# Moving the buffers of a TensorE-filled kernel to other offsets modulo 512 bytes

## The chip, the cores and the metric

The kernel runs on one NeuronCore of one Trainium2 chip. The metric is the device time of one execution in microseconds (us). A program that runs on one core has one span, and the profile shows one execution of it.

## The reference

Three layers follow one another, all in float32: a sparse attention, and two gated feed-forward layers on its output.

```python
def _attn_ref(q, k, v):                      # each 4 x 8 x 576 x 64
    scores = scale * np.matmul(q, k.transpose(0, 1, 3, 2))
    rel = pos[:, None] - pos[None, :]
    mask_local = (rel >= 0) & (rel < 32)                       # heads 0 to 3
    mask_strided = (rel >= 0) & (pos[None, :] % 32 == pos[:, None] % 32)   # heads 4 to 7
    ...
    return np.matmul(attn, v)                # softmax of the masked scores, times v

def _moe_ref(x, w_a, w_b, w_out):            # x 2304 x 512, w_a and w_b 512 x 1536
    return (x @ w_a) * (x @ w_b) @ w_out

def _moe2_ref(x, w_gate, w_val, w_out):      # the same shapes
    return 1.0 / (1.0 + np.exp(-(x @ w_gate))) * (x @ w_val) @ w_out
```

The result is `_moe2_ref(_moe_ref(_attn_ref(q, k, v)))`, 2304 tokens by 512.

## The kernel before, in words

**Precision.** Every large product is made of three matmuls in float32r, a 4-byte type that TensorE takes at one column per cycle: high part of the weights by high part of the data, low by high, high by low. So each operand lies in SBUF twice, as a high and a low part. The stationary operand of a matmul (its weights) is always 128 by 128; the moving operand is 512, 384 or 256 columns wide. Each matmul has its own weight load, and the load of the next matmul runs while the current one streams.

**Stages.** (1) Tokens come in five tiles: four of 512 columns (128 positions of 4 sequences) and a last one of 256. For each tile the attention is computed (local heads on TensorE at L569, L610 and L624, strided heads by VectorE at L787 to L857, their transposes at L883), and then the first layer runs over 12 slices of its inner dimension: per slice 24 matmuls at L929 (two products of 4 chunks by 3 parts) and 12 at L1020 (the output product). That gives 4 x 12 x 24 = 1,152 matmuls at L929 and 4 x 12 x 12 = 576 at L1020 that are 512 wide, and 288 and 144 that are 256 wide. Attention and strided heads of the next tile run beside the first layer of the current one. (2) The second layer's gate and value products, and (3) its output product, use a seven-product scheme for blocks of two by two; all their matmuls are 384 wide and issue from L1299: 3 x 6 x 14 x 6 = 1,512 in stage 2 and 3 x 14 x 18 = 756 in stage 3, 2,268 in all. At the very start, while there is little to do, TensorE is fed with bf16 matmuls of zeros (L429, tile `nil`), 512 wide.

**Order.** A planner (`Plan`) sorts all operations of all engines by costs and due times before anything is issued, and the program is written out in that order. TensorE's large matmuls are tied in one chain by `chain`.

**Memory.** SBUF is addressed by column numbers. The columns up to F0 are cut into 17 zones: `w0` to `w11` of 12,288 bytes per partition, which hold the first layer's weights; `x12` to `x15` of 8,192 bytes, which hold the tokens (`x12`, `x13` high parts, `x14`, `x15` low parts); and `h16` of 4,096 bytes for the features between the first layer's two products. In stages 2 and 3 the same zones hold weights and moving operands of the second layer, in other roles. What lies behind F0 is in one tile, `rest`. The function `at` turns a column number into a view, and makes a zone's tile (`sb.tile`, with one tag per zone) when the zone is first used. The allocator packs tiles in the order in which they are first made.

**Start addresses.** All pieces inside the zones begin at multiples of 512 bytes from the zone's start, with one exception: the tokens and features of the last, 256 wide, tile begin 192 bytes further (`SHIFT = 48` columns, in `token_column` and `gated`). In the kernel before, every zone begins at 384 modulo 512 bytes. So the first column of a moving operand and the first column of the weights that are loaded meanwhile have the same address modulo 512 in all 512 and 384 wide matmuls, and are 192 bytes apart in the 256 wide ones. Below, that distance (moving operand's start minus the start of the next matmul's weights, modulo 512) is called the offset.

Of the kernel before, what the change touches and what calls it, by code (L numbers as in the profile page):

```python
# [7 lines left out]
F32 = mybir.dt.float32  # L8
# [14 lines left out]
P = 128  # L23
KC = DM // P
KF = DFF // P
# [44 lines left out]
REGIONS = [(i * ZONE, ZONE) for i in range(KF)]  # L70
# [3 lines left out]
REGIONS += [(H0, 2 * N2)]  # L74
F0 = H0 + 2 * N2
EARLY, FIRST, SECOND, THIRD = range(4)
RINGS = {"c": (8, DM), "qk": (2, QW + KW), "g": (1, N2), "raw": (3, T * D), "hh": (1, N2), "hl": (1, N2)}
PLACE, TOP = {"hh": H0, "hl": H0 + N2}, F0
for _n, (_k, _w) in RINGS.items():
    if _n not in PLACE:  # L80
# [4 lines left out]
def region_of(a):  # L85
    return next((r for r in REGIONS if r[0] <= a < r[0] + r[1]), None)
# [86 lines left out]
class Plan:  # L173
# [39 lines left out]
    def add(self, eng, cost, fn, deps=(), key=0.0, take=(), free=(), size=0):  # L213
# [7 lines left out]
        for ring, owner in free:  # L221
            if ring in PLACE:
                taker, i = owner if isinstance(owner, tuple) else (owner, None)
                rings = [allowed for r, allowed in taker.take if r == ring]
                for allowed in rings if i is None else rings[i:i + 1]:
                    size = RINGS[ring][1]
                    for s in allowed:
# [124 lines left out]
def attention_moe_kernel(ctx, tc, qkv, sq, sk, sv, w1, w2, mask, ident, out):  # L352
# [4 lines left out]
    sb = ctx.enter_context(tc.tile_pool(name="sb", bufs=1))  # L357
# [10 lines left out]
    tiles = {}  # L368

    def at(a, n, phase=FIRST, dtype=F32):  # L370
        r = region_of(a)
        if r is None:
            v = rest[:, a - F0:a - F0 + n]
        else:
            if tiles.get(r, (None,))[0] != phase:
                name = f"{('w', 'x', 'h')[(r[0] >= X0) + (r[0] >= H0)]}{REGIONS.index(r)}"
                tiles[r] = phase, sb.tile([P, r[1]], F32, tag=name, name=f"{name}p{phase}")
            v = tiles[r][1][:, a - r[0]:a - r[0] + n]
        return v if dtype == F32 else v.bitcast(dtype)

    def xT(i, c):

        return at(X0 + (2 * i + c // 2) * XZONE, XZONE, FIRST, F32R).rearrange("p (c n) -> p c n", c=HK)
# [5 lines left out]
    def buf(op, ring, shape, dtype=F32):  # L389
        s = op.slot[ring][0]  # L390
        if ring in PLACE:
            return at(PLACE[ring] + s * RINGS[ring][1], shape[1], FIRST, dtype)
        return sb.tile(shape, dtype, tag=f"{ring}{s}", name=f"{ring}{s}")
# [65 lines left out]
    def convert(w, need, start=()):  # L459
# [3 lines left out]
        def clear(op):  # L463
            for i in op.slot["c"]:
                tops.append(at(PLACE["c"] + i * DM, DM, FIRST, U32))
                POOL.memset(tops[-1], 0)
# [567 lines left out]
    for i, n in enumerate(TILES):  # L1034
        n *= B
        war = reads1[-1:]
        w = [g for g in GROUPS if g.i == i + 1]
# [563 lines left out]
```

## Time and profile before

| what | value |
|---|---|
| median of 2 runs | 903.11 us (902.96 to 903.26) |
| the profiled execution | 902.92 us, of which 901.1 us is the span from the first to the last instruction |
| TensorE (PE) busy | 892.8 us, 99% |
| VectorE (DVE) busy | 655.1 us, 73% |
| ScalarE (ACT) busy | 405.0 us, 45% |
| DMA | 132.67 MB, 147 GB/s on average |

PE stands for TensorE's matmuls, PEld for its weight loads, which overlap them. A matmul's duration in the profile is its way through the array and not the time that it costs in a row of matmuls: that time is the distance between the starts of two of them, and it can be read where the chain that ended last lists a number of matmuls with their joint time.

### The profile page before, as it was taken

How to read it: one execution, taken by the hardware profiler on the slowest of the kernel's cores; microseconds unless marked ns; L12 is line 12 of the kernel's file. 1: busy time of each engine (PE TensorE's matmuls, PEld its weight loads, DVE VectorE, ACT ScalarE, POOL GpSimd, SP SyncE). 2: the span in 40 equal slices, each digit the busy share in tenths (PEclk: the TensorE clock that was granted, in tenths of full speed). 3: DMA queues.
4: the chain of work that ended last, by engine and by line, in shares of the span. 5: the costliest groups of instructions: out<-in, count | busy, mean ns of one | idle time of the engine just before them, and what ended most of it. 6: DMA issues, size and time to landing. Idle time of an engine off the chain costs nothing.

```text
span 901.1 us, 13664 instructions
## 1 busy us (share of the span) xinstructions
PE 892.8 (99%) x5170; PEld 802.0 (89%) x5170; DVE 655.1 (73%) x1078; ACT 405.0 (45%) x843; POOL 11.4 (1%) x23
## 2 busy tenths in 40 slices
PE   8999999999999999999999999999999999999998
PEld 4678888888888888888899999999999999999998
DVE  7999988998999879811328876675768458649481
ACT  5776644411242113311236655564656445435351
POOL 4000000000000000000000000000000000000000
PEclk9999999999999999999999999999999999999999
DMA  9676564311242124300034233645575588953501
GB/s 297 212 238 221 200 195 141 91 44 61 85 137 72 54 65 134 106 1 1 0 118 164 94 139 116 213 152 187 204 241 169 194 302 331 381 165 117 167 17 62
DMA packets 62513, 132.67 MB, mean 147 GB/s; under 512 B 5872, under 2 KB 37232, under 8 KB 61552
## 3 DMA queue, kind: packets, MB, share of 16 engines
q1 hardware_dynamic: 62160, 131.60, 43.7%
q8 instruction: 40, 0.66, 0.3%
q14 instruction: 25, 0.20, 0.1%
q10 hardware_dynamic: 288, 0.21, 0.1%
HBM read 97.19 MB, written 34.60 MB: 146 GB/s over the span
## 4 chain that ended last, share of the span: by engine, by line
PE 97%; DVE 3%; issue 0%; ACT 0%; DVEq 0%
PE bank L1299 43%; PE bank L929 33%; PE bank L1020 17%; PE bank L624 1%; PE idle L429 1%; PE bank L569 1%; PE bank L610 1%; PE bank L883 0%; DVE nm L581 0%; DVE rest L497 0%; PE bank L442 0%; DVE w8p L857 0%; DVE w9p L857 0%; DVE x14p L636 0%; DVE w4p L1255 0%; DVE w0p L509 0%
## 5 line engine op out<-in xcount | busy, mean ns | idle before, releaser
L954 ACT CAST h16p<-rest 128x512 fp32r<-128x512 f32 (+1 forms) x60 | 34.7, 578 | 143.7 <-PE bank L1020 140.5
L1311 DVE TENSOR_TENSOR rest<-bank,rest 128x384 f32<-128x384 f32 x84 | 46.3, 555 | 56.6 <-PE bank L1299 32.5
L950 DVE TENSOR_TENSOR rest<-bank,rest 128x512 f32<-128x512 f32 (+1 forms) x60 | 38.1, 635 | 53.7 <-PE bank L929 53.5
L1072 ACT COPY rest<-bank 128x512 f32<-128x512 f32 (+1 forms) x60 | 32.6, 544 | 92.2 <-PE bank L929 92.0
L1317 ACT COPY rest<-bank 128x384 f32<-128x384 f32 x84 | 40.2, 479 | 67.4 <-PE bank L1299 67.1
L958 DVE TENSOR_TENSOR h16p<-rest,h16p 128x512 fp32r<-128x512 f32 (+1 forms) x60 | 38.2, 636 | 28.8 <-PE bank L1020 23.5
L787 DVE TENSOR_TENSOR rest<-rest 128x320 f32<-128x320 f32 (+13 forms) x56 | 51.5, 920 | 1.3 <-DMA rest<-sq 0.5
L850 DVE TENSOR_TENSOR rest<-rest,s 128x320 f32<-128x320 f32 (+13 forms) x56 | 51.5, 920 | 0.9
L793 DVE TENSOR_REDUCE s<-rest 128x5 f32<-128x320 f32 (+13 forms) x56 | 51.2, 915 | 1.2
L857 DVE TENSOR_REDUCE rest<-rest 128x64 f32<-128x320 f32 (+13 forms) x56 | 51.2, 915 | 1.0
L488 ACT ACTIVATE rest<-rest 128x512 f16<-128x512 bf16 x36 | 28.4, 793 | 9.4 <-DMA rest<-w 9.1
L1209 DVE SCALAR_TENSOR_TENSOR rest<-rest 128x512 uint32<-128x512 uint32 x36 | 24.7, 688 | 9.9 <-ACT rest L1202 9.8
L1202 ACT ACTIVATE rest<-rest 128x512 f16<-128x512 bf16 x36 | 28.0, 788 | 5.5 <-DMA rest<-w 5.5
L1382 DVE TENSOR_TENSOR rest<-bank,rest 128x384 f32<-128x384 f32 x36 | 20.0, 556 | 12.1 <-PE bank L1299 11.4
L1321 ACT COPY bank<-bank 128x384 f32<-128x384 f32 x42 | 19.6, 466 | 18.6 <-PE bank L1299 18.3
L1376 ACT ACTIVATE rest<-bank 128x384 f32<-128x384 f32 x36 | 17.6, 490 | 22.3 <-PE bank L1299 22.1
L497 DVE SCALAR_TENSOR_TENSOR rest<-rest 128x512 uint32<-128x512 uint32 x36 | 24.5, 685 | 0.6 <-ACT rest L488 0.5
L587 ACT ACTIVATE rest<-bank,nm 128x96 f32<-128x96 f32 x56 | 18.3, 338 | 12.2 <-DVE nm L582 10.7
L1376 ACT ACTIVATE rest<-rest 128x768 f32<-128x768 f32 x18 | 15.2, 846 | 14.0 <-DVE rest L1311 13.7
L1299 PE MATMUL bank<-w8p,w10p 128*128 128x384 f32 x100 | 20.7, 334 | 0.0
L1382 DVE TENSOR_TENSOR rest<-rest 128x768 f32<-128x768 f32 x18 | 17.2, 954 | 0.7 <-ACT rest L1376 0.3
L1299 PEld LDWEIGHTS bank<-w8p,w10p 128*128 128x128 f32 x100 | 17.6, 188 | 0.0
(500 smaller groups left out, 2413.7 us busy)
## 6 DMA issues: line engine op xcount, KB each, us to landing
rest<-w SPq DMA_DIRECT2D x72, 511.8 KB, 3.9
h2d<-rest SPq DMA_DIRECT2D x18, 768.0 KB, 4.2
rest<-qkv SPq DMA_DIRECT2D x12, 416.0 KB, 4.0
w2p<-h2d SPq DMA_DIRECT2D x12, 384.0 KB, 4.6
w0p<-h2d SPq DMA_DIRECT2D x12, 384.0 KB, 5.0
w1p<-h2d SPq DMA_DIRECT2D x12, 384.0 KB, 5.5
out<-rest SPq DMA_DIRECT2D x24, 192.0 KB, 1.8
x2d<-rest SPq DMA_DIRECT2D x16, 256.0 KB, 2.1
```

Of the source, the lines that this page charges most:

```text
L787: engine[op.eng].tensor_tensor(out=product(op, n), in0=x["k", h][:, :, :n, :], in1=x["q"][h // 2][:, e:e + nh, j:j + 1, :].to_broadcast([P ...
L793: DVE.tensor_reduce(out=weights_of(h, j, n), in_=x["p", op.deps[0]], op=ALU.add, axis=AX.X)
L850: engine[op.eng].tensor_tensor(out=product(op, n, "p (h d t) -> p h d t"), in0=x["v", h][:, :, :, :n], in1=weights_of(h, j, n).unsqueeze(2 ...
L857: DVE.tensor_reduce(out=xs[:, j, e:e + nh, :], in_=x["p", op.deps[0]], op=ALU.add, axis=AX.X)
L929: PE.matmul(x[tag][:, :n], ww[:, c * P:(c + 1) * P], xx(c), start=(u == 0 and c == chunks[0]), stop=(u == last and c == chunks[-1]),)
L950: DVE.tensor_tensor(out=x["g"], in0=x["b"][:, :n], in1=x["g"], op=ALU.mult)
L958: DVE.tensor_tensor(out=x["hl"], in0=x["g"], in1=r32(x["hh"]), op=ALU.subtract)
L1020: PE.matmul(ps[:, :n], ww[:, m * P:(m + 1) * P], x[xx], start=start, stop=stop)
L1299: PE.matmul(bank_of(where), at(*lhs(a, (0, 1, 0)[q], c), F32R), at(*rhs(b, (0, 0, 1)[q], c), F32R), start=p in OPENS and (q, c) == units[0 ...
L1311: DVE.tensor_tensor(out=at(*o), in0=bank_of("Z"), in1=at(*a), op=ALU.add)
L1317: "ACT", act2(NS), lambda op: ACT.copy(out=at(*o), in_=bank_of("Y")), [ops[after]], key - 20))
L1382: DVE.tensor_tensor(out=at(*o), in0=src(), in1=at(*o), op=ALU.mult)
```

## The change

The zones are made ahead of everything else, in a fixed order (`PLACED`), and some of them get a few columns more than they use (`PADS`), so that the next zone begins elsewhere modulo 512 bytes. All columns are used as before, and each engine executes the same instructions, in the same order and with the same waits; only addresses differ. `FRONT`, which is 0, adds nothing.

```diff
@@ -74,6 +74,11 @@
 EARLY, FIRST, SECOND, THIRD = range(4)
+PLACED = ["x12", "x13", "x14", "h16", "x15"] + [f"w{i}" for i in range(KF)]
+PADS = {"x12": 48, "x13": 32, "h16": 32} | {f"w{i}": 16 for i in range(7)}
+FRONT = 0
@@ -374,9 +379,14 @@
-                tiles[r] = phase, sb.tile([P, r[1]], F32, tag=name, name=f"{name}p{phase}")
+                tiles[r] = phase, sb.tile([P, r[1] + PADS.get(name, 0)], F32, tag=name, name=f"{name}p{phase}")
...
+    if FRONT:
+        sb.tile([P, FRONT], F32, name="front")
+    for name in PLACED:
+        at(REGIONS[int(name[1:])][0], 1, EARLY)
```

The allocation that follows, start modulo 512 bytes:

| zone | before | after |
|---|---|---|
| x12, x13 (tokens, high) | 384, 384 | 0, 192 |
| x14, x15 (tokens, low) | 384, 384 | 320, 448 |
| h16 (features) | 384 | 320 |
| w0, w1, w2, w3 | 384 each | 448, 0, 64, 128 |
| w4, w5, w6 | 384 each | 192, 256, 320 |
| w7 to w11 | 384 each | 384 each |

Counted over the program, the offset of a matmul to the weights loaded behind it falls out like this after the change (in per cent of the matmuls of that width; before, 100% at 0, 100% at 0 and 100% at 192):

| offset | 0 | 64 | 128 | 192 | 256 | 320 | 384 | 448 |
|---|---|---|---|---|---|---|---|---|
| 512 wide | 8 | 12 | 16 | 8 | 8 | 16 | 8 | 23 |
| 384 wide | 18 | 12 | 16 | 17 | 11 | 11 | 6 | 9 |
| 256 wide | 16 | 8 | 23 | 8 | 12 | 16 | 8 | 8 |

## Rows read from the trace of the kernel before

**Rows 1.** The page: busy time per engine, and the TensorE clock granted per slice.
```profile
span 901.1 us, 13664 instructions
...
PE 892.8 (99%) x5170; PEld 802.0 (89%) x5170; DVE 655.1 (73%) x1078; ACT 405.0 (45%) x843; POOL 11.4 (1%) x23
...
PEclk9999999999999999999999999999999999999999
```

**Rows 2.** The page: the chain that ended last, by engine and by line.
```profile
PE 97%; DVE 3%; issue 0%; ACT 0%; DVEq 0%
PE bank L1299 43%; PE bank L929 33%; PE bank L1020 17%; PE bank L624 1%; PE idle L429 1%; PE bank L569 1%; PE bank L610 1%; PE bank L883 0%; DVE nm L581 0%; DVE rest L497 0%; PE bank L442 0%; DVE w8p L857 0%; DVE w9p L857 0%; DVE x14p L636 0%; DVE w4p L1255 0%; DVE w0p L509 0%
```

**Rows 3.** The chain in order of time, stage 1: start us, us, what.
```profile
440.50 5.44 PE bank L929 x24
445.94 2.72 PE bank L1020 x12
...
479.65 2.83 PE bank L929 x24
482.48 1.41 PE bank L1020 x12
```

**Rows 4.** The same, stages 2 and 3, the two longest pieces.
```profile
503.01 43.70 PE bank L1299 x252
551.57 346.26 PE bank L1299 x1996
```

**Rows 5.** The same, the bf16 matmuls of zeros, 7.3 to 9.2 us.
```profile
7.23 2.16 PE idle L429 x10
```

**Rows 6.** The same, four float32 transposes at 170 us.
```profile
170.62 0.44 PE bank L610 x4
```

**Rows 7.** Busy time in stretches: us, then busy us (x count) of PE, PEld, DVE, ACT, POOL, clock, DMA.
```profile
25.00:75.00 50.00, 48.39 (x325) 37.83 (x325) 47.44 (x97) 36.42 (x87) 0.00 (x0) 1.00 0.70 224
75.00:130.00 55.00, 55.00 (x247) 45.54 (x246) 53.10 (x97) 33.24 (x53) 0.26 (x1) 1.00 0.57 191
130.00:240.00 110.00, 110.00 (x603) 90.19 (x602) 99.41 (x142) 31.31 (x82) 0.31 (x1) 1.00 0.31 95
...
552.00:740.00 188.00, 188.00 (x1087) 188.00 (x1086) 120.79 (x239) 107.14 (x209) 0.00 (x0) 1.00 0.60 203
```

**Rows 8.** Weight loads (PEld) of two lines: busy us, mean ns of one.
```profile
L1299 PEld LDWEIGHTS bank<-w8p,w10p 128*128 128x128 f32 x100 | 17.6, 188 | 0.0
...
L883 PEld LDWEIGHTS bank<-idt,rest 128*128 128x128 f32 x28 | 3.5, 140 | 1.1
```

**Rows 9.** The chain in order of time between the two pieces of rows 4.
```profile
546.74 0.56 DVE rest L1311
...
550.29 1.23 DVE w4p L1255
```

## Prediction

> **What bounds the kernel now.** I read the page first. TensorE is busy for 892.8 of 901.1 us and its clock is granted in full in every slice [rows 1], so this is a kernel that ends when TensorE has worked off its matmuls. The chain that ended last says the same by line: L1299, L929 and L1020, the three lines with the float32r matmuls, hold 93% of the span, and everything on VectorE together 3% [rows 2]. No idle time is left to win and no instruction is moved. So the change can act in one way only: through the time that one matmul takes from its start to the start of the next.
>
> That time stands in the chain in order of time, where a run of matmuls has a count and a joint time. L929 with 512 columns: 5.44 us for 24, or 226.7 ns; L1020 with 512 columns: 2.72 for 12, the same. In the last tile, with 256 columns, 2.83 for 24 is 117.9 and 1.41 for 12 is 117.5 [rows 3]. Stages 2 and 3: 346.26 us for 1,996 is 173.5 ns at 384 columns, and 43.70 for 252 is 173.4 [rows 4]. At the full clock, 2.4 GHz by the granted clock, the columns alone take 213.3, 160.0 and 106.7 ns. What a matmul costs beyond its columns is then 13.4 ns at 512, 13.5 ns at 384, and 11.0 ns at 256. For a yardstick, the bf16 matmuls of zeros, also 512 wide, take 2.16 us for 10, or 216.0 ns: 2.7 ns beyond their columns [rows 5]. So float32r pays some 10.7 ns per matmul that bf16 does not pay, and the question of this case is how much of it hangs on where the two operands lie.
>
> **The change, part by part.** It removes, adds and moves no instruction, no transfer and no wait, so none has a price; that part is 0. Of the 17 zones 12 (x12 to x15, h16, w0 to w6) get another place modulo 512, and for the matmuls that matter the offset between moving operand and next weights stops being 0: 92% of the 1,728 matmuls of 512 columns and 82% of the 2,268 of 384 columns go to another offset, while 16% of the 432 of 256 columns, now at 192, go to 0. The other engines read and write the same zones at other places too; with VectorE at 73% and ScalarE at 45% [rows 1] I cost that at nothing, and TensorE's work hides it.
>
> *The price of the offset.* The trace has one pair of rows in which it differs: 512 and 384 columns run at offset 0 and pay 13.4 and 13.5 ns, 256 columns run at 192 and pay 11.0 [rows 3, 4]. The first two are alike although their widths differ by 128 columns, so a price by width does not offer itself, and a lower price by offset does: 2.4 to 2.5 ns per matmul. The bounds are wide. No gain: the 256 wide matmul may owe its 11.0 ns to its width alone. Largest gain: all that bf16 does not pay, 10.7 ns at 512, 10.8 at 384 and, for the matmuls of the last tile that find a cheap offset, 8.3. Loss: nothing excludes that other offsets cost more than 0 does, since only 192 was ever run. I take the value from the nearest rows, 2.4 ns, because they are the same instruction with the same load beside it; the bf16 rows differ in type and have zeros as data.
>
> Sum by that value: 1,728 x 0.92 x 2.4 = 3.8 us, and 2,268 x 0.82 x 2.5 = 4.6 us; back go 432 x 0.16 x 2.4 = 0.2 us. That is 8.2 us. Set against the profiled execution (901.1 us span, 1.8 us around it, 902.9 in all) it leaves 894.7, and against the median of 903.1 it leaves 895.
>
> *What could eat the gain.* In the first tiles VectorE is nearly full too: 47.44 of 50 and 53.10 of 55 us [rows 7]. A TensorE that is 1% faster needs 104 instead of 105 us there, against 100.5 us of VectorE, so the gain stays; one that is 4.7% faster (10.7 of 226.7 ns) needs 100 us and meets VectorE's own work. From 130 us on VectorE has 10% of room, and in stage 2 a third [rows 7]. Between the two long runs of L1299 the chain goes through VectorE and ScalarE for 4.9 us [rows 4, 9]; that stretch gains nothing, which is 0.05 us.
>
> **The rivals.** *A: part of the cost goes, as above,* 895 us.
>
> *B: the offset is no cost.* Weight load and moving operand may never meet. For it: the four transposes in a row at 170 us follow each other at 110 ns [rows 6], with weights that lie 384 bytes apart in turn, so at four different offsets to the same moving identity, and the other transposes look the same; nor do the weight loads say anything of being stretched, 188 ns each [rows 8]. Against it: a float32 transpose takes those 110 ns for 128 columns, half the pace, so its moving operand leaves every second slot free, and its load takes 140 ns, not 188 [rows 8]; and the 13.4 and 13.5 against 11.0 ns stay unexplained. The time is that of now, 903. The Trainium skill ("SBUF — State Buffer", Who interferes with whom, and the section on the bandwidth pool) says this outright: TensorE has one read port for the moving operand and another for weight loads, and never waits on anyone. By that rule the change does nothing, 903 us; the float32r rows, which pay 10.7 ns that bf16 does not, do not refute it, since the type could cost that by itself.
>
> *C: nearly all of the cost goes.* Two streams that start at the same place modulo 512 bytes, 3,996 times, is what a collision would need to be at its worst, and then only 18% or less of the matmuls would keep it. For it: the 256 wide matmul, at 117.5 ns, may be held by something else, such as its own weight load, which at 188 ns is longer than the whole distance [rows 8], so that its 11.0 ns hides a price of the offset that is lower still. Whole: 1,728 x 0.92 x 10.7 = 17.0, 2,268 x 0.82 x 10.8 = 20.1, 432 x 0.84 x 8.3 = 3.0, together 40.1 us, less some 2 us for VectorE's full stretch: 865. Half of it: 884. Against it: the seven other offsets would all have to be cheap. The Trainium skill's price for a matmul of 512 columns in a row ("TensorE: Matmul & The Clock Gate", Back-to-back issue gap) is N / 2.4 + 2.5, or 215.8 ns, which is what the bf16 rows show and the float32r rows do not.
>
> *D: other offsets are dearer than 0, and it gets slower.* The place is the weight load beside a stream. With offset 0 both start together, and the moving operand, which takes a column per cycle, draws ahead of a load that needs longer; if it starts behind the load's place instead (offsets 256 to 448), it would run into it. Those offsets hold 55% of the 512 wide and 37% of the 384 wide matmuls. Were they to pay the 13.4 ns twice: 1,728 x 0.55 x 13.4 + 2,268 x 0.37 x 13.5 = 12.7 + 11.3 = 24 us, 927 us. It decides from 4.5 ns more per matmul on (18 us over 3,996). For it: nothing in the rows prices those offsets. Against it: the one other offset that was run, 192, is cheaper and not dearer.
>
> That the change does not do what it says is no rival: the allocation shows the places.
>
> **How the numbers follow.** A 0.34, B 0.30, C 0.24, D 0.12. The prediction is A's 895. The range has to hold 8 in 10: A and B and the nearer part of C, from 868 (C's whole effect, less a little) to 906 (B with 0.3% of noise and secondary effects); left out are D's larger part and the last bit of C, about 0.19. What a measurement of this kernel can tell from no change is taken as 2%, 18 us: faster than 885 is nearly all of C and none of A, 0.24; slower than 921 is D's larger part, 0.10; the rest, with A and B in it, is 0.66.
>
> **What would show it right or wrong.** After the change, the joint times in the chain are the test. A: L929 with 24 of 512 columns takes 5.38 to 5.40 us in place of 5.44, and L1299 shows 171 to 172 ns; slices where tokens and weights happen to keep offset 0 (w1 against x12, w4 against x13, w6 against h16) stay at 226.7. B: all rows as they were. C: slices below 5.3 us, and between 25 and 130 us waits of TensorE for VectorE. D: distances that differ from slice to slice, some over 230 ns. I would be most wrong if the distance depended on the absolute place of one operand and not on the offset between two, since then the one pair of rows that I price from says nothing about the other places.

## The result, and the profile after

The changed kernel takes 913.33 us (912.74 to 913.91, 2 runs) against 903.11: a ratio of 1.0113, with a 95% interval of 1.0070 to 1.0157. It is slower by 10.2 us, where 8.2 us less had been forecast, and outside the range of 868 to 906.

The page of the kernel after (busy time per engine, granted clock per slice) shows that TensorE's own time grew: its matmuls are busy for 902.5 us in place of 892.8, with the same number of them and the full clock, while VectorE and ScalarE stay within 1 us of before [rows 1].

```profile
span 911.0 us, 13664 instructions
...
PE 902.5 (99%) x5170; PEld 804.9 (88%) x5170; DVE 655.9 (72%) x1078; ACT 405.3 (44%) x843; POOL 11.6 (1%) x23
...
PEclk9999999999999999999999999999999999999999
```

The chain that ended last, in order of time, is where the time can be seen (start us, us, what). The file is ten lines longer, so L929, L1020 and L1299 are now L939, L1030 and L1309. First some slices of stage 1, then one of the last tile, then stages 2 and 3:

```profile
191.50 5.55 PE bank L939 x24
197.05 2.77 PE bank L1030 x12
...
205.37 2.72 PE bank L1030 x12
...
214.08 2.80 PE bank L1030 x12
216.88 5.54 PE bank L939 x24
...
490.78 2.87 PE bank L939 x24
493.64 1.42 PE bank L1030 x12
...
510.01 44.05 PE bank L1309 x252
...
558.94 348.70 PE bank L1309 x1996
```

Before, 24 product matmuls took 5.44 us in every undisturbed slice and 12 output matmuls 2.72 [rows 3]. Now the products take 5.54 to 5.55, and the output matmuls depend on the slice: 2.77 with the weights of `w5` (offset 64), 2.72 with `w6` (offset 0), 2.80 with `w7` (offset 448). So the same instruction, in the same program, with its features in the same place, has three prices, and at offset 0 it has its old one. The product matmuls are another matter: their offset changes every two matmuls, and those at offset 0 or 256 among them do not keep the old price. By the distances of their starts (stalls over 260 ns left out), 175 such matmuls took 231.4 ns on average, hardly another time than those at offset 64 (230.2), 128 (231.4) and 192 (232.3), all modulo 256. In the last tile the prices scatter around the old ones (2.87 for 2.83, 1.42 for 1.41). Stage 1 ends 7.0 us later (the first run of L1309 starts at 510.01 instead of 503.01), and the two runs of stages 2 and 3 are 0.35 and 2.44 us longer [rows 4]; that is 9.8 of the 9.9 us by which the span grew. The chain through VectorE and ScalarE between them [rows 9] lasts 4.9 us as it did, and TensorE's waits are those of before.

### The profile page after: what moved, and what is told of

Read it like the earlier page. It is cut to its first block, busy times and chain, and to the rows that moved or that the text cites. A ratio compares the mean times of both kernels' runs of the same rounds, so it can differ in the third digit from the quotient of the medians.

```text
span 911.0 us, 13664 instructions
## 1 busy us (share of the span) xinstructions
PE 902.5 (99%) x5170; PEld 804.9 (88%) x5170; DVE 655.9 (72%) x1078; ACT 405.3 (44%) x843; POOL 11.6 (1%) x23
## 4 chain that ended last, share of the span: by engine, by line
PE 97%; DVE 3%; issue 0%; ACT 0%; DVEq 0%
PE bank L1309 43%; PE bank L939 33%; PE bank L1030 17%; PE bank L634 1%; PE idle L439 1%; PE bank L579 1%; PE bank L620 1%; PE bank L893 0%; DVE nm L591 0%; DVE rest L507 0%; PE bank L452 0%; DVE w8p L867 0%; DVE w9p L867 0%; DVE x14p L646 0%; DVE w4p L1265 0%
## 5 line engine op out<-in xcount | busy, mean ns | idle before, releaser
L1309 PE MATMUL bank<-w8p,w10p 128*128 128x384 f32 x100 | 20.8, 336 | 0.0
L1309 PEld LDWEIGHTS bank<-w8p,w10p 128*128 128x128 f32 x100 | 17.7, 188 | 0.0
L1309 PE MATMUL bank<-x15p,w3p 128*128 128x384 f32 x88 | 17.5, 336 | 0.0
```

Of the source, the lines that this page charges most:

```text
L1309: PE.matmul(bank_of(where), at(*lhs(a, (0, 1, 0)[q], c), F32R), at(*rhs(b, (0, 0, 1)[q], c), F32R), start=p in OPENS and (q, c) == units[0 ...
```

## The experiments

Three theories were set against each other. *Pair*: a matmul's time is set by the offset between its moving operand and the weights beside it. *Place*: it is set by where an operand lies by itself, or by the new order of the zones. *Switch*: it is the change of the offset from one matmul to the next that costs, and not the offset. All runs use the changed kernel's fixed order of zones unless the text says otherwise. Those with tokens and features mapped to other offsets, the one without the shift and the two with a shift of a few columns were executed once, the others 4 to 10 times; all but one of the 33 times of the kernel before that were taken beside them lie between 902.46 and 904.57, so a difference of a microsecond in one execution says nothing. The kernel before had a median of 903.02 us beside the first four (19 runs), 902.46 beside the next four (one run), and 903.42 beside the last four (13 runs).

**All zones at another place, offset 0.**

```diff
-PADS = {"x12": 48, "x13": 32, "h16": 32} | {f"w{i}": 16 for i in range(7)}
-FRONT = 0
+PADS = {}
+FRONT = 48
```

> All 17 zones begin at 192 modulo 512, in the fixed order of the changed kernel, without gaps; offset 0 between moving operand and next weights everywhere, as before. Pair theory (the offset between the two decides): 903, runs of 24 matmuls of 512 columns at 5.44 us, 384 columns at 173.4 ns. Place theory (the absolute place modulo 512, or the new order of the zones, decides): not 903; with all zones moved away from 384 up to the 913 of the changed kernel. Switch theory (the offset changing from one matmul to the next costs): 903, since nothing changes.

It took 903.26 us, a ratio of 1.0003 (0.9994 to 1.0013), with runs of 24 at 5.44. The chain in order of time of this kernel:

```profile
190.54 5.44 PE bank L939 x24
...
553.19 346.26 PE bank L1309 x1996
```

Every operand has moved by 320 bytes modulo 512 and the zones have a new order, and each row has its old time to a hundredth of a microsecond. The place theory falls, as far as a place at a multiple of 64 bytes goes: this run has no other.

**Weights 256 bytes away.**

```diff
+PADS = {"x15": 64}
```

> Tokens and features at 0, all weight zones at 256, so offset 256 in all 512 wide matmuls, 0 or 256 in the 384 wide. Pair theory with a period of 256 bytes (the changed kernel has steady 226 to 227 ns at offset 256 as well as at 0): 903, runs of 24 at 5.44 us. Pair theory with a period of 512, in which 256 is as dear as the mean of the others: 910 to 913, runs at 5.52. Switch theory: 903.

It took 903.61 us, a ratio of 1.0005 (0.9995 to 1.0015). The chain:

```profile
191.50 5.44 PE bank L939 x24
```

So 256 is as good as 0. What counts is the offset modulo 256, not modulo 512; runs below agree, with 2.75 us per 12 at both 64 and 320, and 2.79 and 2.80 at 128 and 384.

**Weights 128 bytes away.**

```diff
+PADS = {"x15": 32}
```

> Tokens and features at 0, all weight zones at 128, so offset 384 in all 512 wide matmuls and in 18% of the 384 wide. Pair theory, with the 229 and 238 ns in turn that the changed kernel shows at offsets 128 and 384: 1,728 x 6.9 = 11.9 us and under 1 us in the 384 wide, 915 to 916, runs of 24 at 5.60 us and of 12 at 2.80. Switch theory: the offset never changes within stage 1, so 903 and 5.44.

It took 913.71 us, a ratio of 1.0115 (1.0099 to 1.0131), as slow as the whole change. The chain:

```profile
216.38 2.80 PE bank L1030 x12
219.18 5.60 PE bank L939 x24
...
561.77 348.06 PE bank L1309 x1996
```

Within the 512 wide matmuls of this kernel no offset ever changes, and they still take 233.3 ns here (232.1 in the slices that run at 5.57). Switching is not needed for the loss; of the three theories only the pair theory gives this. It had said 915 to 916: its price of 6.9 ns was somewhat too high for the 512 wide matmuls, and its "under 1 us" too low for the 384 wide ones, whose longer run alone lost 1.8 us (348.06 for 346.26 [rows 4]).

**Half of the change: tokens and features.**

```diff
-PADS = {"x12": 48, "x13": 32, "h16": 32} | {f"w{i}": 16 for i in range(7)}
+PADS = {"x12": 48, "x13": 32, "h16": 32, "x15": 112}
```

> Half of the change: tokens and features where the changed kernel has them, all weight zones at 384. Offsets of the 512 wide matmuls 448 (45%), 128 (23%), 320 (22%), 64 (11%), none at 0; 384 wide at 0 in 73%. Pair theory: 755 x 6.8 + 383 x 6.9 + 545 x 2.3 ns = 9.0 us, 912, with runs of 24 at 5.54 and of 12 at 2.80. Theory that spreading the weights is what costs: 903. Switch theory: tokens still alternate, so half or more of the loss, 908 to 913, but the features, which have one offset, stay at 2.72 per 12.

It took 911.59 us, a ratio of 1.0097 (1.0078 to 1.0115), with runs of 24 at 5.54 and of 12 at 2.80:

```profile
88.85 2.80 PE bank L1030 x12
91.65 5.54 PE bank L939 x24
```

The theory that only the spread weights cost falls.

**The other half: weights.**

```diff
+PADS = {"x15": 16} | {f"w{i}": 16 for i in range(7)}
+FRONT = 96
```

> The other half of the change: the weight zones at the eight places of the changed kernel, tokens and features all at 384. By the price of each offset (64: 2.3 to 2.7 ns, 128 and 192: 6.7, 0: none, with a period of 256) the 144 matmuls of 512 columns per slice give 144 x (6.8 + 6.7 + 2.3 + 0 + 6.8 + 6.7 + 2.3) ns = 4.6 us; the 384 wide, by the changed kernel's means at their offsets, 3.2 us: 911. If the loss of the two halves simply added up to the changed kernel's 10.2 us, this one would be left 10.2 - 8.6 = 1.6 us, 905.

It took 909.88 us, a ratio of 1.0068 (1.0053 to 1.0083). The chain, with weights `w5`, `w6` and `w7` (offsets 128, 64 and 0) in the three output rows:

```profile
197.16 2.79 PE bank L1030 x12
...
205.41 2.75 PE bank L1030 x12
...
214.06 2.72 PE bank L1030 x12
```

Beside the changed kernel this separates pair and place once more: the weights in `w6` begin at 320 in both kernels and cost 2.72 us per 12 with features at 320 but 2.75 with features at 384, and those in `w7`, at 384 in both, cost 2.80 and 2.72. It had been put at 911. The two halves lose 8.6 and 6.5 us and the whole change 10.2, so they do not add up: where both operands move, what counts is the distance that is left between them.

**Other offsets, to map the price.** The next three put tokens and features at different offsets, so that each run gives two prices, one for the products and one for the output product. Here the features' zone is placed behind the tokens' (`x12`, `x13`, `x14`, `x15`, `h16`).

```diff
+PADS = {"x15": 48, "h16": 56}     # products 96, output 288
```

> Weight zones at 416, tokens at 0, features at 192, so the 512 wide matmuls of the products have offset 96 throughout and those of the output product 288 (32 in a period of 256). Theory that 0 is the bottom of a valley: by a straight line between the prices at 64-byte steps (226.7 ns at 0, 229 at 64, 233.5 at 128 and 192) 231.3 and 227.9 ns, 1,152 x 4.6 + 576 x 1.2 ns = 6 us, 909. Theory that only steps of 64 count (eight places of 64 bytes): 32 as dear as 0 or 64, 96 as dear as 64 or 128. Theory that a finer offset is cheaper than 0: a run of 12 of the output product under 2.72 us.

It took 915.26 us, and the valley had said 909. The chain:

```profile
224.62 2.80 PE bank L1030 x12
227.41 5.60 PE bank L939 x24
```

Offset 32 costs as much as 96 or 128: 233.3 ns. There is no slope down to 0. In this run and the next the weights begin 32 bytes off a multiple of 64. That this costs by itself was not tested at 512 columns; at 384 columns it does not, since the 1,561 matmuls with both operands in weight zones, and so at offset 0, take 173.8 and 173.6 ns in these two runs and 173.8 in the run after them, where all zones lie at multiples of 64.

```diff
+PADS = {"x15": 16, "h16": 8}      # products 416, output 480
```

> As before it, with offset 160 for the products (416, less a period of 256) and 224 for the output product. Valley: 233.5 and 230.1 ns, 1,152 x 6.8 + 576 x 3.4 ns = 9.8 us, 913. Theory that a finer offset is cheaper than 0: a run of 12 of the output product under 2.72 us.

It took 917.09 us, the longest time of all layouts; the valley had said 913. The chain:

```profile
224.71 2.80 PE bank L1030 x12
227.51 5.61 PE bank L939 x24
```

```diff
+PADS = {"x15": 32, "h16": 48}     # products 192, output 320
```

> Offset 192 for the 512 wide matmuls of the products, the one place from which the prediction priced all others, and 320 (64 in a period of 256) for the output product. The prediction's step (192 is 2.4 ns cheaper than 0 at every width): 224.3 ns, runs of 24 at 5.38, 899 to 900. Pair theory with the price set by width and offset together: 231 and 236 ns in turn, runs of 24 at 5.60, runs of 12 of the output product at 2.75; 1,152 x 6.8 + 576 x 2.3 ns = 9.2 us, 912.

It took 912.62 us. The chain:

```profile
223.99 2.75 PE bank L1030 x12
226.74 5.59 PE bank L939 x24
```

At offset 192, from which the prediction had taken its price, a 512 wide matmul takes 232.9 ns, 6.2 more than at 0 and not 2.4 less. At 384 columns, 376 matmuls of this run lie at offset 192 too; by the distances of their starts they take 173.0 ns, where the same ones took 173.3 in the kernel before: 0.3 ns less and not 2.5. At 512 columns offset 64 costs 229.2 ns and is the cheapest after 0.

**The last tile without its shift.** This is the kernel before with one number changed.

```diff
-SHIFT = 48
+SHIFT = 0
```

> The kernel before with the last tile's 192-byte shift taken away (offset 0 in the 256 wide matmuls too). Prediction's step (0 costs 13.4 ns beyond the columns at any width): 120.1 ns, runs of 24 at 2.88 us, 432 x 2.2 ns = 1 us, 904. Theory that the 256 wide matmul is shorter for its width alone: 117.9 ns, 2.83 us, 903.

It took 903.39 us where the kernel before took 902.46, one execution each, so only the rows can tell. The chain, 256 columns:

```profile
475.38 2.88 PE bank L929 x24
```

That is 120.0 ns, where 117.9 was read at 192 [rows 3]: at 256 columns the shift does save 2.1 ns per matmul.

**A shift of one column, and of four.** The features begin one column further inside their zone (the zone has 64 more columns, to keep all zones at 0 or 256), and in the second run the tokens four columns.

```diff
+PADS = {"h16": 64}
-            v = tiles[r][1][:, a - r[0]:a - r[0] + n]
+            o = a - r[0] + (1 if r[0] >= H0 else 0)
+            v = tiles[r][1][:, o:o + n]
```

> All offsets 0 or 256 as in the run with all zones apart by 256, except that the features of the first layer lie one column (4 bytes) further in their zone: offset 260, 4 in a period of 256, for the 576 output matmuls of 512 columns. Notch theory (only the exact same place, in steps of a line of some 16 or more bytes, is cheap; 32 already costs 232.8 ns): 4 bytes are still the same line, runs of 12 at 2.72, 903. Theory that the very same column is what is cheap: as at 32, 232.8 ns, 2.79, 576 x 6 ns = 3.5 us, 906. Theory that 0 is itself a collision and a finer offset is cheaper: under 2.72, under 902.

It took 909.62 us. The chain (two more lines in the file):

```profile
225.38 5.45 PE bank L940 x24
230.83 2.84 PE bank L1031 x12
...
473.31 2.74 PE bank L940 x24
477.49 2.83 PE bank L940 x24
```

Four bytes beside the same place make 236.7 ns of 226.7, the highest price found. So the theory that a common line of 16 bytes is enough falls: what was found cheap is the same column modulo 256 bytes. Here and in the next run, though, one operand alone left the multiples of 64 bytes, and no run moved both operands by 4 or 16 bytes together. Whether such a start costs by itself, apart from the offset, was not tested.

```diff
+PADS = {"x12": 64, "x13": 64, "x14": 64, "x15": 64}
+            o = a - r[0] + (4 if H0 > r[0] >= X0 else 0)
```

> Tokens four columns (16 bytes) further in their zones, all zones at 0 or 256: offset 16 in a period of 256 for the 1,152 product matmuls of 512 columns, 0 for the output matmuls. Notch no wider than 16 bytes: as at 32, 232.8 ns, runs of 24 at 5.59, 1,152 x 6 ns = 6.9 us, 910. Notch between 16 and 32 bytes wide: 5.44 and 903. Finer offset cheaper: under 5.44.

It took 908.80 us. The chain:

```profile
224.21 5.56 PE bank L940 x24
229.77 2.75 PE bank L1031 x12
...
474.95 1.36 PE bank L1031 x12
```

16 bytes cost 231.7 ns, so the cheap place is no wider than that, and by the run before not even four bytes wide. The output matmuls in these rows are at offset 0, and yet 12 of them take 2.75 us, 229.2 ns each, and not 2.72: by the starts in the trace the first six behind the products take 231.4 ns on average and the other six 227.5. So the offset of a matmul alone does not set its time; what went before it still tells for some matmuls. No offset that was tried goes under 226.7 ns at 512 columns.

**A version that might beat both.** At 256 columns offset 32 looked a little better than 192, so this is the kernel before with that shift.

```diff
-SHIFT = 48
+SHIFT = 8
```

> The kernel before with the last tile 32 bytes from its zone's start in place of 192. Runs of 24 matmuls of 256 columns took 2.80 us at offset 288 (32 in a period of 256) where tokens had it, against 2.83: 288 x 1.2 ns = 0.35 us and up to 0.2 us more in the output product, 902.6 where the kernel before has 903.1. If it is the neighbours' mixture of offsets that made 2.80, no change or worse.

It took 903.15 us beside 903.42, a ratio of 0.9996 (0.9986 to 1.0006). The chain:

```profile
476.41 2.80 PE bank L929 x24
```

The rows have the 1.2 ns per matmul that was expected, but 0.4 us is less than the time can show. No version beats the kernel before measurably.

## Why the prediction was wrong

**What bounds the kernel** was right. TensorE's distances from matmul to matmul are the whole of it: no wait changed and no other engine got in the way, and 9.8 of 9.9 us of span are in the three runs of matmuls.

**That the offset has a price** was right, and rival B, no effect, falls: with offset 384 in all 512 wide matmuls the ratio was 1.0115, with 256 it was 1.0005. The rule of the Trainium skill ("SBUF — State Buffer", Who interferes with whom) that TensorE never waits on anyone would have given B's 903. Here the same matmul took 226.7 to 236.7 ns with nothing but operands' addresses changed, and the measurement decides. The transposes that spoke for B are at half the pace, as the prediction noted against them.

**The step that failed is "the price of the offset"**, the value of 2.4 ns by which offsets other than 0 were to be cheaper at every width. Its reading of the rows was sound as far as it went: 256 columns at offset 0 do cost 120.0 ns, 13.3 beyond their columns, just as 512 and 384 columns cost 13.4 and 13.5, and the last tile's shift is what brought them to 11.0. What failed is the carrying over of one offset, at one width, to seven offsets at two other widths. At 192 itself, the one offset that was priced, 512 columns cost 6.2 ns more than at 0, and 384 columns only 0.3 less. The prices depend on the width and the offset together. For 512 columns they read as follows where the offset stays the same over a run of 24 or 12:

| offset modulo 256 | 0 | 4 | 16 | 32 | 64 | 96 | 128 | 160 | 192 | 224 |
|---|---|---|---|---|---|---|---|---|---|---|
| 512 columns, ns | 226.7 | 236.7 | 231.7 | 233.3 | 229.2 | 233.3 | 233.3 | 233.8 | 232.9 | 233.3 |

At 512 columns 0 is the cheapest of the ten, and the change's other offsets, all multiples of 64, lose 2.5 to 6.6 ns there, 256 excepted. At 256 columns 0 is dearer than 32 and 192. So the sign of the sum was wrong for its 1,590 matmuls of 512 columns that left offset 0: they were to gain 3.8 us, and stage 1 ended 7.0 us later. In stages 2 and 3 the change lost 2.8 us where 4.6 had been forecast as gain.

**Rival D** had the direction, with a chance of 0.12, but not the mechanism. Its place, offsets 256 to 448, is refuted by 256, which costs nothing, and by 64, which does; its price of 13.4 ns was twice what was found, and so it had 24 us for 10.2.

**Rival C**, that two operands which begin at the same place are the worst case, had it the wrong way round: they are the best case at 512 columns. That all matmuls pay some 13.4 ns at offset 0, where bf16 pays 2.7 [rows 5], stays unexplained, and no offset tried took it away at 512 columns.

**The range** came from cases that gain or do nothing. The prediction said that nothing excludes a loss, and then let one row against it, the 256 wide one, decide how likely that was.

**What stays open** is how the two operands disturb each other. The price repeats every 256 bytes, at the offsets where that was tried (0, 64 and 128), and in runs of one offset it is set by that offset; but whether the partner is the weights that are loaded during the matmul or its own was not separated, as both lie at the same offset nearly everywhere. That the load beside the stream is what meets it was only argued. Open is also what carries over from one matmul to the next: in the changed kernel, whose products mix their offsets, a matmul's own offset hardly tells its time, so the table gives the loss of such a mixture at most on average.

## What to carry to other kernels

Where matmuls follow each other without a gap, read the time of one from a run of them in the chain, per line and width, before and after any change of layout: an allocation alone moved it by 1 to 4% here, with the same instructions and waits. Do not carry the price of one alignment to another width; measure it at the width in question, with all zones at one offset, as one pad does. In this kernel the plain layout, in which all zones begin at the same place modulo 256 bytes, was the best of those tried for its 512 wide matmuls, and spreading the buffers over eight places cost 1.1%.

## What the runs showed of the hardware that had not been expected

- The offset counts modulo 256 bytes: 0 and 256 both give 5.44 us per 24 matmuls of 512 columns, 64 and 320 both 2.75 per 12.
- A shift of one operand by a single column, 4 bytes, is the dearest found: 2.84 us per 12 against 2.72.
- At offset 0 a float32r matmul costs the same beyond its columns at all three widths: 13.4, 13.5 and 13.3 ns at 512, 384 and 256.
- One offset can have more than one pace. At 512 columns offset 0 took 2.72 us per 12 in the kernel before and 2.75 behind products that were 16 bytes off. At 256 columns it is plainer. The output matmuls of the last tile at offset 192 took 1.41 us per 12 in the kernel before [rows 3] and 1.36 us where the tokens ahead of them lay 16 bytes further; the products took 2.83 per 24 there, but in the run with the features one column off 2.74 in five slices and 2.83 in seven, at the same offset and in one execution. In the fast slices the matmuls follow each other at 113 to 114 ns on average from the first few on to the end of the run, and at 118 in the others. So the 11.0 ns that the prediction read at 192 were one of two paces there, the other being some 7. What happened before a run of matmuls seems to last into it; this was not followed up.
